# Three w1 chunks in the ring where there were four, and 1,728 fewer columns of one record loaded again

## The chip, the cores and the metric

The program runs on one core of one Trainium2 chip. The metric is device time in microseconds (us): 711.79 us is the median of three runs of the kernel before (711.76 to 711.85). Times inside the program come from one profiled execution.

## What is computed

Two layers are applied twice in turn to four tokens of 640 values: attention over a cached window (32 heads of 128, the last 1,024 keys and values of a cache of 4,096), then a dense layer of width 1,728 with a ReLU. Everything is float32. Cut to what matters:

```python
def _A_ref(x, k_cache, v_cache, wq, wo):        # k, v: the last W = 1024 of 4096 positions
    q = (x @ wq).reshape(B, Sq, Hq, Dh).transpose(0, 2, 1, 3)
    scores = jnp.einsum("bhqd,bhkd->bhqk", q, k) * (Dh ** -0.5)
    p = _softmax(scores, axis=-1)
    o = jnp.einsum("bhqk,bhkd->bhqd", p, v)
    return o.transpose(0, 2, 1, 3).reshape(B, Sq, Hq * Dh) @ wo

def _B_ref(x, w1, w2):
    h = jnp.maximum(jnp.einsum("bsd,df->bsf", x, w1), 0)
    return jnp.einsum("bsf,fd->bsd", h, w2)

x = x + _A_ref(_layernorm(x), A_k_cache, A_v_cache, A_wq, A_wo)   # round one
x = x + _B_ref(_layernorm(x), B_w1, B_w2)
x = x + _A_ref(_layernorm(x), A_k_cache, A_v_cache, A_wq, A_wo)   # round two, same weights and caches
x = x + _B_ref(_layernorm(x), B_w1, B_w2)
```

## The kernel before

All weights and caches of one head lie side by side as a record of 9,472 columns by 128 partitions: wq (640 columns), keys (4,096), values (4,096), wo (640). One column is 512 bytes over all partitions, so a record is 4.85 MB. The kernel streams records from memory into five slots of one record each. TensorE (PE) forms a head's query, its scores, its values and its share of the projection; VectorE (DVE) and ScalarE (ACT) do the softmax. After 32 heads the dense layer (`mlp`) runs on w1 (8,640 columns, five chunks of 1,728, each a block of 128 rows of the input) and w2 (54 tiles of 160 columns). Then the same again as round two.

Both rounds read the same records, so what is still on the chip at the end of round one isn't loaded again. Five records (heads 27 to 31) stay in the slots and come first in round two. A sixth (head 26, `SIXTH`) comes next; it lives in `ring`, a buffer of 9,152 columns beside the slots. Between its two uses, round one's w1 and w2 have to pass through the low columns of the same ring. The columns from `KEPT` (6,944) upwards are left alone; 1,056 columns just below `KEPT` (and 320 at the ring's start) are moved aside into PSUM (`put_by`, `lend`) and copied back later (`take_back` by ACT, in the dense layer; `put_back` by DVE, in round two). What lies below `HELD` (5,888) is overwritten and is loaded again, in the four pieces of `SIXTH_PIECES`.

What passes through the ring is the table `MLP_RING`: one entry for each load, with its quarters of a w1 chunk, its w2 tiles and the ring column where it starts. Every load is one DMA on the queue of SyncE (SP), which issues in the order of the list `items` and waits at each entry until the columns that it overwrites were last read (`pump`, `free`, `done`); the loads behind it wait too. A load that overwrites a w1 chunk waits for that chunk's last matmul. Four chunks fit before, at columns 0, 1,728, 3,456 and 5,184; the fifth takes the first one's place. Then come the w2 loads, the pieces of the sixth record, and the first loads of round two into the slots, each of which waits until PE has read what it overwrites.

PE's order is the order of the code. `busy(n)` is a filler: a product of one row with n columns whose result nobody reads. It writes columns 512 and up of `sc_ps[1]`; the 512 columns that `lend` put aside lie in the same tile `sc_ps[1]`, and `take_back` reads them there. In `mlp`, round one, there is a filler behind the tiles of w2 loads 1, 2 and 3 (counted from 0), and `take_back` comes behind load 2. Right behind the last w2 tile DVE transposes the new x, and PE starts on round two: the query of head 27 (`center`, `query`), then its scores.

All recorded operations have the line of one helper (`InOrder`, line 94), so the profile's rows are told apart by their tiles.

Of the kernel before, what the change touches and what calls it, by code (L numbers as in the profile page):

```python
# [2 lines left out]

# [12 lines left out]
B, D, H, DH, W, FF = 4, 640, 32, 128, 1024, 1728  # L41
# [20 lines left out]
SIXTH = H - NS - 1  # L62
RING = WO + 2 * FD
W1_COLS = KB * FF
KEPT = 4 * FF + 32
LENT = 512
BESIDE = KEPT - 192 - (512 - FD)
HELD = BESIDE - LENT

MLP_RING = [(4, 0, 0), (4, 0, FF), (4, 0, 2 * FF), (4, 0, 3 * FF), (4, 0, 0), (0, 10, 1728), (0, 11, 3328), (0, 11, 5088),  # L70
            (0, 10, 0), (0, 8, 1600), (0, 4, 2880)]

SIXTH_PIECES = [(3520, 5088), (5088, HELD), (0, 1600), (1600, 3520)]
FILL = [False, False, False, True]
W1_SLOT = [[0, 1], [2], [3], [4]]
W2_SLOT = [22, 14, 10, 4, 4]
# [25 lines left out]
def decode_kernel(ctx: ExitStack, tc: tile.TileContext, xf, rec, w, out):  # L102
# [65 lines left out]
    def home(h, r):  # L168

        if h == SIXTH:  # L170
            return "ring"
        return h % NS if not r or h >= LAST else (h + LAST) % NS
# [10 lines left out]
    def load(key, src, lo, hi, buf, col):  # L183
        buf, col = place(buf, col)
        items.append(([(key, lo, hi, col)] if key else [], src, lo, hi, buf, col))
# [33 lines left out]
    n = 0  # L219
    for quarters, tiles, col in MLP_RING:  # L220
        size = quarters * FQ + tiles * FD
# [3 lines left out]

    for lo, hi in SIXTH_PIECES:
        load(None, rec[:, SIXTH * REC:], lo, hi, "ring", lo)
# [19 lines left out]
    def pump():  # L247

        while items:
            parts, src, lo, hi, buf, col = items[0]  # L250
            if any(b == buf and x < col + hi - lo and col < y for b, x, y in live):
                return
            sp.dma_start(buffers[buf][:, col:col + hi - lo], src[:, lo:hi])
            live.append((buf, col, col + hi - lo))
            for key, x, y, c in parts:
                at.setdefault(key, []).append((x, y, buf, c))
            items.pop(0)
# [4 lines left out]
    def cols(key, lo, n):  # L262

        for x, y, buf, col in pieces(key):
            if x <= lo and lo + n <= y:
                return buffers[buf][:, col + lo - x:col + lo - x + n]
        raise KeyError((key, lo, n))

    def free(buf, a, b):
        rest = []  # L270
        for bb, u, v in live:
            if bb != buf or v <= a or b <= u:
                rest.append((bb, u, v))
            else:
                rest += [(bb, p, q) for p, q in ((u, a), (b, v)) if p < q]
        live[:] = rest

    def done(key, lo, hi):

        if key[0] == "rec" and key[1] == 0 and key[2] >= LAST:  # L280
            return
        if key == ("rec", 0, SIXTH):
            hi = min(hi, HELD)
        for x, y, buf, col in pieces(key):
            a, b = col + max(lo, x) - x, col + min(hi, y) - x
            if a < b:
                free(buf, a, b)
        pump()

    aside = acc[:, FD:], ring[:, BESIDE:BESIDE + 512 - FD]  # L290
    held = [(0, 0, REC - RING), (REC - RING, BESIDE + 512 - FD, KEPT)]
    lent = sc_ps[1][:, :LENT], ring[:, HELD:BESIDE]

    def put_by():

        for col, a, b in held:
            dve.tensor_copy(hold[:, col:col + b - a], ring[:, a:b])
            free("ring", a, b)
        free("ring", BESIDE, KEPT)
        pump()  # L300
# [7 lines left out]
    def take_back():  # L308

        assert not any(buf == "ring" and x < BESIDE and HELD < y for buf, x, y in live), live  # L310
        act.activation(*lent[::-1], AF.Copy)
        live.append(("ring", HELD, BESIDE))
# [10 lines left out]
    def busy(n, to=sc_ps[1][:, 512:]):  # L323

        pe.matmul(to[0:1, :n], ones, slot[home(LAST, 0)][:, K:K + n], start=True, stop=True)

    def centered_wq(h, ks):

        mean = sc_ps[1][:, 512:512 + DH]
        for k in ks:  # L330
            pe.matmul(mean, minus.to_broadcast([P, P]), cols(("rec", 0, h), WQ + k * DH, DH), start=(k == 0),
                      stop=(k == KB - 1))
        if ks[-1] == KB - 1:
            wq = cols(("rec", 0, h), WQ, D).rearrange("p (k d) -> p k d", d=DH)
            dve.tensor_tensor(wq, wq, mean.unsqueeze(1).to_broadcast([P, KB, DH]), op=OP.add)
# [27 lines left out]
    def deviation(bias, scale):  # L363

        pe.matmul(o_ps[:, 8:8 + B], ones.to_broadcast([P, P]), squares, start=True, stop=True)
        act.activation(rstds, o_ps[:, 8:8 + B], AF.Sqrt, bias=bias, scale=scale / D)

    def row_rstd(rows):

        dve.reciprocal(rstds, rstds)  # L370
        dve.tensor_tensor(mrt, rstds, rows, op=OP.mult)
        dve.tensor_reduce(rstd, mrt, op=OP.add, axis=AX.X)

    def xblock(k):
        return xT[:, 32 * k:32 * k + B]
# [58 lines left out]
    def picks(last, copy=None):  # L434
        o = outs[last].rearrange("p (c j) -> p c j", c=4)
        dve.tensor_tensor(o, o, of_block.unsqueeze(2).to_broadcast([P, 4, DH]), op=OP.mult)
        if copy:
            dve.tensor_copy(*copy)
        dve.tensor_reduce(on[last], o.rearrange("p c j -> p j c"), op=OP.add, axis=AX.X)
# [12 lines left out]
    def mlp(r):  # L452


        h_ps, front, back = sc_ps[0][:, :512], t_ps[:, :224], sc_ps[0][:, 512:768]
        key = ("w", r)
        turns = list(accumulate(quarters for quarters, _, _ in MLP_RING if quarters))
        for n in range(KB * NB):
            k, j = divmod(n, NB)
            pe.matmul(h_ps[32 * j:32 * j + B, :FQ], xblock(k), cols(key, n * FQ, FQ), start=(k == 0),  # L460
                      stop=(k == KB - 1))
            done(key, n * FQ, n * FQ + FQ)
            if n == NB - 1:
                deviation(eps, 1.0)
                if r == 0:
                    busy(256)
                row_rstd(pick)
            if r == 0 and n + 1 in turns[:-1]:
                i = turns.index(n + 1)
                if i in (1, 2):  # L470
                    centered_wq(LAST, (range(0, 2), range(2, KB))[i - 1])
                elif FILL[i]:
                    busy(512)
        act.activation(front, h_ps[:, :224], AF.Relu, scale=rstd)
        act.activation(back[:, :208], h_ps[:, 224:FQ], AF.Relu, scale=rstd)
        act.activation(back[:, 240:], h_ps[:, 416:FQ], AF.Relu, scale=rstd)
        dve.transpose(scratch[:, :224], front)
        dve.transpose(scratch[:, 224:], back)
        busy(512)
        busy(256)  # L480
        sizes = W2_SLOT if r else [tiles for _, tiles, _ in MLP_RING if tiles]
        first = 0
        for i, size in enumerate(sizes):
            for s in range(first, first + size):
                m, n = TILES[s]
                w2 = cols(key, W1_COLS + s * FD, FD)
                for part, q in ((m, n),) if m < 13 else ((13, n), (14, n + 2)):
                    pe.matmul(acc[32 * q:32 * q + B, :FD], hT[:, part, :B], w2,
                              start=False, stop=(s >= len(TILES) - NB), skip_group_check=True)
            if r == 0 and 0 < i < len(sizes) - 2:  # L490
                busy(512)
            done(key, W1_COLS + first * FD, W1_COLS + (first + size) * FD)
            if r == 0 and i == 2:
                take_back()
            first += size


    pump()
    pe.matmul(acc[:, :FD], ident, x_sb, start=True, stop=False, skip_group_check=True)
    for r in range(2):  # L500
# [11 lines left out]
        for n, h in enumerate(hs[:-2]):  # L512
            i = n - (H - late)
# [5 lines left out]
            if back:  # L519
                assert not any(buf == "ring" and x < KEPT and BESIDE < y for buf, x, y in live)  # L520
            picks(0, aside[::-1] if back else aside if r == 0 and h == SIXTH else None)
# [30 lines left out]
        for i in (late - 3, late - 1, late - 2) if late > 2 else (1,):  # L552
            project(r, hs[H - late + i], i, i == late - 2 or late == 2)
        center()
        mlp(r)
    dve.tensor_copy(x_sb, acc[:, :FD])
    sp.dma_start(out, x_sb)
# [38 lines left out]
```

## Time and profile before

| | |
|---|---|
| median of three runs | 711.79 us (711.76 to 711.85) |
| profiled execution, first to last instruction (span) | 710.5 us |
| between that span and the median of the runs | 1.3 us |
| PE, DVE, ACT busy | 72%, 46%, 14% of the span |
| DMA traffic | 302.64 MB, mean 426 GB/s |
| read from memory by the program's own loads | 302.00 MB |
| round one's dense layer | about 366 to 385 us |

The profile gives the profiled execution's span only; its whole device time isn't shown, so the runs' median stands beside the span. The rows of the windows view give a stretch of time (us from the span's start), its length, the busy time of PE, PE's weight load, DVE, ACT and POOL with the number of instructions, the granted clock of TensorE (1.00 is full speed), the busy share of the 16 DMA engines, and the GB/s that they moved. A DMA engine counts as busy from a packet's start to its end, also while the packet waits. "us to landing" runs from the issue on SP to the last of a load's bytes being reported. KB are 1,024 bytes.

### The profile page before, as it was taken

What the parts mean: (1) busy time and instruction counts of PE and PEld (TensorE: products, weight loads), DVE (VectorE), ACT (ScalarE), POOL (GpSimd) and SP (SyncE); (2) the same over time, 40 slices, a digit from 0 to 9 for tenths busy, and PEclk for the clock granted to TensorE, in tenths of its full rate; (3) what the DMA queues carried; (4) which work ended last, traced back from release to release, by engine and by line L of the source; (5) the groups of instructions that cost most, each with busy time, mean ns of one, the idle gap of its engine ahead of it and who ended that gap; (6) DMA issues with size and microseconds to landing.
All of it is one profiled execution on the core that took longest, in us unless ns stands there. A gap on an engine that the chain in (4) does not pass through costs nothing.

```text
span 710.5 us, 8690 instructions
## 1 busy us (share of the span) xinstructions
PE 513.6 (72%) x3706; PEld 202.8 (29%) x3706; DVE 323.3 (46%) x678; ACT 99.7 (14%) x211; POOL 1.1 (0%) x9
## 2 busy tenths in 40 slices
PE   3567686678584578857888898865686677576897
PEld 2132232232231223322223334331331322231423
DVE  3333353353452353546641777644352444253762
ACT  1100110011010110111121212201010111011111
POOL 0000000000000000000000000000000000000000
PEclk9957787677777776888999899977576677677899
DMA  9999999999999999999999999999999999999997
GB/s 381 463 409 451 415 442 443 414 442 444 424 429 440 434 429 421 435 425 430 424 416 403 421 435 428 438 434 448 429 445 427 428 442 430 427 442 406 431 423 292
DMA packets 13318, 302.64 MB, mean 426 GB/s; under 512 B 1488, under 2 KB 1760, under 8 KB 5216
## 3 DMA queue, kind: packets, MB, share of 16 engines
q1 hardware_dynamic: 13248, 302.08, 99.1%
q8 instruction: 29, 0.48, 0.2%
q14 instruction: 9, 0.07, 0.0%
q10 hardware_dynamic: 32, 0.01, 0.0%
HBM read 302.00 MB, written 0.08 MB: 425 GB/s over the span
## 4 chain that ended last, share of the span: by engine, by line
DMA 73%; PE 21%; DVE 4%; issue 1%; ACT 1%; SPq 0%; ACTq 0%; DVEq 0%
DMA slots<-rec 57%; PE sc_ps L94 11%; DMA ring<-w 8%; PE o_ps L94 7%; DMA ring<-rec 5%; PE acc L94 2%; DMA slots<-w 2%; DVE scratch L94 2%; DVE o_ps L94 1%; ACT oTs L94 1%; DVE small L94 0%; ACT sc_ps L94 0%; DVE turned L94 0%; SPq L94 0%; DVE ring L94 0%
## 5 line engine op out<-in xcount | busy, mean ns | idle before, releaser
L94 PE MATMUL sc_ps<-slots,qT 128*4 128x512 f32 x992 | 194.5, 869 | 37.4 <-DMA slots<-rec 36.4
L94 PE MATMUL sc_ps<-xT,slots 128*128 128x4 f32 x620 | 94.6, 279 | 99.8 <-DMA slots<-rec 99.2
L94 PE MATMUL o_ps<-slots,scratch 128*16 128x512 f32 x960 | 149.3, 693 | 2.4 <-DVE scratch L94 1.7
L94 DVE TENSOR_REDUCE small<-sc_ps 128x1 f32<-128x1024 f32 x64 | 78.3, 1224 | 156.9 <-PE sc_ps L94 156.9
L94 PEld LDWEIGHTS sc_ps<-xT,slots 128*128 128x128 f32 x620 | 89.2, 225 | 157.8 <-DMA slots<-rec 109.0
L94 ACT ACTIVATE sc_ps<-sc_ps,small 128x1024 f32<-128x1024 f32 (+1 forms) x68 | 71.1, 1046 | 342.2 <-DVE small L94 340.7
L94 DVE STREAM_TRANSPOSE turned<-sc_ps 128x1024 f32<-128x1024 f32 (+1 forms) x85 | 84.6, 996 | 0.7
L94 PEld LDWEIGHTS o_ps<-slots,scratch 128*16 128x16 f32 x960 | 34.5, 118 | 120.0 <-issue 107.6
L94 DVE TENSOR_TENSOR o_ps<-o_ps,of_block 128x512 f32<-128x512 f32 x62 | 43.4, 699 | 53.6 <-PE o_ps L94 52.3
L94 PEld LDWEIGHTS sc_ps<-slots,qT 128*4 128x4 f32 x992 | 32.3, 108 | 121.9 <-issue 64.9
L94 DVE TENSOR_TENSOR qT<-sc_ps,by_row 128x4 f32<-128x4 f32 x62 | 9.7, 156 | 114.1 <-PE sc_ps L94 114.1
L94 PE MATMUL acc<-slots,oTs 128*4 128x160 f32 x496 | 35.4, 368 | 19.2 <-ACT oTs L94 18.5
L94 DVE TENSOR_REDUCE scratch<-o_ps 128x128 f32<-128x512 f32 x62 | 42.9, 691 | 2.1
L94 ACT ACTIVATE oTs<-o_ps 128x4 f32<-128x4 f32 x64 | 11.1, 174 | 214.1 <-PE o_ps L94 214.1
L94 PE MATMUL o_ps<-pick,scratch 128*128 128x4 f32 x128 | 26.8, 280 | 15.9 <-DVE scratch L94 15.9
L94 PEld LDWEIGHTS o_ps<-pick,scratch 128*128 128x128 f32 x128 | 22.4, 218 | 21.4 <-DVE scratch L94 21.1
L94 DVE TENSOR_TENSOR scratch<-turned,by_row 128x128 f32<-128x128 f32 (+1 forms) x85 | 22.0, 259 | 3.2
L94 PE MATMUL sc_ps<-slots,small 128*1 128x512 f32 (+2 forms) x56 | 21.5, 486 | 0.0
L94 DVE TENSOR_SCALAR by_row<-of_batch,small 128x4 f32<-128x4 f32 x64 | 14.7, 230 | 2.2
L94 PEld LDWEIGHTS acc<-slots,oTs 128*4 128x4 f32 x496 | 6.9, 84 | 25.2 <-ACT oTs L94 23.5
L94 DVE STREAM_TRANSPOSE scratch<-small 128x32 f32<-128x32 f32 x64 | 12.9, 202 | 2.2 <-ACT sc_ps L94 2.2
L94 ACT ACTIVATION_READ_ACCUMULATOR sc_ps<-sc_ps,small 128x1 f32 x64 | 12.3, 193 | 0.0
(66 smaller groups left out, 103.7 us busy)
## 6 DMA issues: line engine op xcount, KB each, us to landing
slots<-rec SPq DMA_DIRECT2D x15, 7872.0 KB, 27.0
slots<-rec SPq DMA_DIRECT2D x8, 7936.0 KB, 31.5
slots<-rec SPq DMA_DIRECT2D x17, 2368.0 KB, 16.9
slots<-rec SPq DMA_DIRECT2D x4, 4736.0 KB, 25.9
slots<-rec SPq DMA_DIRECT2D x2, 4416.0 KB, 29.3
slots<-rec SPq DMA_DIRECT2D x7, 1024.0 KB, 19.7
ring<-w SPq DMA_DIRECT2D x8, 864.0 KB, 10.9
ring<-rec SPq DMA_DIRECT2D x1, 4576.0 KB, 36.2
```

Of the source, the lines that this page charges most:

```text
L94: r = build(*args, **kwargs)
```

## The change

Columns up to `KEPT` = 5,216 are now given to the stream, so three w1 chunks fit (at 0, 1,728 and 3,456) and the fourth waits for the first. The 1,056 columns that are moved aside lie at 4,160 to 5,216. Round two loads columns 0 to 4,160 of the sixth record again, in pieces of 1,600, 800, 1,120 and 640. The w2 loads hold 11, 10, 11, 11, 7 and 4 tiles (before: 10, 11, 11, 10, 8, 4), and `take_back` stands behind w2 load 3. PE gets two more fillers in round one: 512 columns behind the tiles of load 4, ahead of the last load's tiles, and 256 columns behind the last tile. The file is 25 lines shorter at the top, so line 94 is line 69 in it.

```diff
-KEPT = 4 * FF + 32
+KEPT = 3 * FF + 32
...
-MLP_RING = [(4, 0, 0), (4, 0, FF), (4, 0, 2 * FF), (4, 0, 3 * FF), (4, 0, 0), (0, 10, 1728), (0, 11, 3328), (0, 11, 5088),
-            (0, 10, 0), (0, 8, 1600), (0, 4, 2880)]
-
-SIXTH_PIECES = [(3520, 5088), (5088, HELD), (0, 1600), (1600, 3520)]
+MLP_RING = [(4, 0, 0), (4, 0, FF), (4, 0, 2 * FF), (4, 0, 0), (4, 0, FF), (0, 11, 2 * FF), (0, 10, 0), (0, 11, 1600),
+            (0, 11, 3360), (0, 7, 0), (0, 4, 1120)]
+
+SIXTH_PIECES = [(1760, 3360), (3360, HELD), (0, 1120), (1120, 1760)]
...
-            if r == 0 and 0 < i < len(sizes) - 2:
+            if r == 0 and 0 < i < len(sizes) - 1:
                 busy(512)
             done(key, W1_COLS + first * FD, W1_COLS + (first + size) * FD)
-            if r == 0 and i == 2:
+            if r == 0 and i == 3:
                 take_back()
             first += size
+        if r == 0:
+            busy(256)
```

SP's queue from the first w1 chunk to round two's first load into the slots, before (`w` is w1 and then w2, `rec` the records):

```order
L94 DMA ring<-w 128x1728 x5
L94 DMA ring<-w 128x1600
L94 DMA ring<-w 128x1760 x2
L94 DMA ring<-w 128x1600
L94 DMA ring<-w 128x1280
L94 DMA ring<-w 128x640
L94 DMA ring<-rec 128x1568
L94 DMA ring<-rec 128x800
L94 DMA ring<-rec 128x1600
L94 DMA ring<-rec 128x1920
L94 DMA slots<-rec 128x640
```

And with the change:

```order
L69 DMA ring<-w 128x1728 x5
L69 DMA ring<-w 128x1760
L69 DMA ring<-w 128x1600
L69 DMA ring<-w 128x1760 x2
L69 DMA ring<-w 128x1120
L69 DMA ring<-w 128x640
L69 DMA ring<-rec 128x1600
L69 DMA ring<-rec 128x800
L69 DMA ring<-rec 128x1120
L69 DMA ring<-rec 128x640
L69 DMA slots<-rec 128x640
```

The number of loads and the columns of w are the same; the four pieces of the record have 4,160 columns in place of 5,888.

PE from w2 load 3 to round two's first query, before, with what each row waits for (`acc<-ring,scratch` are the w2 tiles, `sc_ps<-slots,small` the fillers, `sc_ps<-xT,slots` the query of head 27; DMAHW is a load, Activation is ACT):

```order
L94 MATMUL acc<-ring,scratch 4x160 [waits DMAHW6_49]
L94 MATMUL acc<-ring,scratch 4x160 x9
L94 MATMUL sc_ps_73<-slots,small 1x512 [waits Activation_49]
L94 MATMUL acc<-ring,scratch 4x160 [waits DMAHW7_49]
L94 MATMUL acc<-ring,scratch 4x160 x7
L94 MATMUL acc<-ring,scratch 4x160 [waits DMAHW0_49]
L94 MATMUL acc<-ring,scratch 4x160 x3
L94 MATMUL sc_ps_72<-xT,slots 128x4 [waits DVE_49]
```

And with the change:

```order
L69 MATMUL acc<-ring,scratch 4x160 [waits DMAHW6_49]
L69 MATMUL acc<-ring,scratch 4x160 x10
L69 MATMUL sc_ps_73<-slots,small 1x512
L69 MATMUL acc<-ring,scratch 4x160 [waits DMAHW7_49]
L69 MATMUL acc<-ring,scratch 4x160 x6
L69 MATMUL sc_ps_73<-slots,small 1x512 [waits Activation_49]
L69 MATMUL acc<-ring,scratch 4x160 [waits DMAHW0_49]
L69 MATMUL acc<-ring,scratch 4x160 x3
L69 MATMUL sc_ps_73<-slots,small 1x256
L69 MATMUL sc_ps_72<-xT,slots 128x4 [waits DVE_49]
```

The filler that waits for ACT's `take_back` moved from behind w2 load 3 to behind load 4, right ahead of the last load's tiles, and a filler stands between the last tile and the query.

## The prediction

> **What bounds the kernel.** I read the page first: how full the DMA engines are, and what the chain that ended last is made of.
>
> ```profile
> span 710.5 us, 8690 instructions
> ...
> DMA  9999999999999999999999999999999999999997
> GB/s 381 463 409 451 415 442 443 414 442 444 424 429 440 434 429 421 435 425 430 424 416 403 421 435 428 438 434 448 429 445 427 428 442 430 427 442 406 431 423 292
> ...
> HBM read 302.00 MB, written 0.08 MB: 425 GB/s over the span
> ...
> DMA 73%; PE 21%; DVE 4%; issue 1%; ACT 1%; SPq 0%; ACTq 0%; DVEq 0%
> ```
>
> The DMA engines are 90% busy or more in every slice but the last, and the chain is DMA for 73%. So the time is about the bytes over the rate, and a byte that is not loaded is time saved, as long as the queue stays fed. Whether it does is read from the stretch that the change touches, the dense layer of round one and what follows it; the windows view, with 500 to 600 us as the steady state:
>
> ```profile
> 350.00:360.00 10.00, 8.86 (x58) 2.77 (x58) 6.91 (x18) 1.98 (x4) 0.00 (x0) 1.00 0.99 414
> 360.00:370.00 10.00, 8.40 (x82) 3.03 (x82) 3.52 (x12) 1.89 (x4) 0.00 (x0) 1.00 1.03 424
> 370.00:380.00 10.00, 8.10 (x80) 2.88 (x80) 1.69 (x3) 1.08 (x3) 0.00 (x0) 1.00 1.01 406
> 380.00:390.00 10.00, 8.90 (x101) 3.84 (x104) 1.33 (x7) 0.80 (x2) 0.00 (x0) 0.88 1.01 397
> 390.00:400.00 10.00, 8.04 (x62) 3.30 (x54) 7.34 (x20) 4.09 (x8) 0.00 (x0) 0.95 1.01 412
> 400.00:410.00 10.00, 9.08 (x68) 3.34 (x72) 6.96 (x16) 1.51 (x4) 0.00 (x0) 0.73 1.03 435
> ...
> 500.00:600.00 100.00, 74.29 (x470) 28.68 (x470) 40.87 (x79) 12.41 (x27) 0.00 (x0) 0.71 1.01 435
> ```
>
> Between 370 and 400 us the busy share says 1.01, yet the rate is 406, 397 and 412 GB/s where it is 435 later. Packets there are held open longer than their bytes need: some of the 16 engines already wait for work with a ring of four. 30 us at a mean of 405 in place of 435 are 2.1 us of transfer. This is the place where the change can lose what it saves.
>
> How the ring feeds the queue is seen in the chain of waits (start, length, what):
>
> ```profile
> 355.18 10.94 DMA ring<-w
> 366.12 0.14 issue
> 366.26 0.91 PE sc_ps L94 x8
> ...
> 367.22 7.14 DMA ring<-w
> 374.37 0.04 issue
> 374.41 0.95 PE sc_ps L94 x8
> ...
> 375.38 7.35 DMA ring<-w
> ...
> 443.23 18.13 DMA slots<-rec
> ```
>
> The first chunk lands at 366.12; PE reads it, and 1.10 us after the landing, at 367.22, the fifth chunk is issued into its place. It lands 7.14 us later, at 374.36. In these 8.24 us four chunks of 864 KB landed, one each 2.06 us, close to the 2.03 us that 884,736 bytes take at 435 GB/s.
>
> **The bytes.** The sixth record's four pieces shrink by 1,728 columns, 884,736 bytes; w1 and w2 are the same 17,280 columns in the same eleven loads, and four pieces stay four. At 435 GB/s that is **-2.03 us**. The lower end by a row, 397 GB/s, gives -2.23.
>
> **The ring of three.** A load into the ring is issued when the chunk three back (before: four back) has been read. One round is then 1.10 us from landing to issue, plus the fixed part of a load (everything but its bytes), plus 2.06 us of bytes, and it has to fit into three transfers, 6.18 us, where it had four, 8.24 us. It fits if the fixed part is no more than 6.18 - 1.10 - 2.06 = **3.02 us**. No row measures the fixed part in this stretch. Bounds are in the DMA issues (KB each, us to landing): the first load of the program, the output at the end, and the loads of w2.
>
> ```profile
> slots<-rec SPq DMA_DIRECT2D x1, 2368.0 KB, 8.3
> ...
> ring<-w SPq DMA_DIRECT2D x2, 880.0 KB, 7.2
> ring<-w SPq DMA_DIRECT2D x2, 800.0 KB, 7.4
> ...
> out<-scratch SPq DMA_DIRECT2D x1, 80.0 KB, 1.6
> ```
>
> The first load finds all engines empty: 8.3 us less 5.57 us for its bytes is 2.7 us. The output is 1.6 less 0.19, 1.4 us, but small and alone. From above, a w2 load of 880 KB lands after 7.2 us of which 2.07 are bytes, so its fixed part is under 5.1. The first load is the nearest kind, a large load for which every engine waits, but nothing else moved then; the fall to 406 GB/s with four chunks says that in traffic some engines wait for longer than that. I take 3.3 us, a quarter of the way from 2.7 to 5.1. That is 0.28 us over per round. From the fourth chunk to the last w2 load eight loads hang on a load three back, 2.7 rounds: **+0.75 us**, between 0 (2.7 us, it fits) and +5.6 (5.1 us).
>
> The Trainium skill (DMA: Bandwidth & Descriptors, section "Anatomy of one DMA — SWDGE (gpsimd) path") has about 2.0 us fixed plus the bytes at 436 GB/s, for the other kind of queue. By it the ring of three would cost nothing. The first load above took 8.3 us where that gives an estimate of 7.6, so the trace is slower than the page.
>
> **The fillers and round two's first loads.** The timeline of w2's end and of round two's start:
>
> ```profile
> 382.47 0.60 ACT L94 ACTIVATE ring<-sc_ps 128x512 f32<-128x512 f32 x1 [5.94 <-PE sc_ps L94]
> ...
> 382.77 0.85 PE L94 MATMUL acc<-ring,scratch 128*4 128x160 f32 x18 [0.34 <-DMA ring<-w]
> 383.33 0.59 PE L94 MATMUL sc_ps<-slots,small 128*1 128x512 f32 x1
> ...
> 383.76 0.59 PE L94 MATMUL sc_ps<-slots,small 128*1 128x512 f32 x1
> 384.31 1.22 PE L94 MATMUL acc<-ring,scratch 128*4 128x160 f32 x24
> 385.90 1.28 PE L94 MATMUL sc_ps<-xT,slots 128*128 128x4 f32 x10 [0.37 <-DVE xT L94]
> ...
> 387.43 1.80 PE L94 MATMUL sc_ps<-slots,qT 128*4 128x512 f32 x8
> ...
> 389.69 1.66 PE L94 MATMUL sc_ps<-slots,qT 128*4 128x512 f32 x8
> ...
> 392.97 1.04 PE L94 MATMUL sc_ps<-slots,qT 128*4 128x512 f32 x8 [0.42 <-DVE qT L94]
> ```
>
> `take_back` on ACT waits for a filler and is waited for by the next one. Before, ACT was done at 383.07, ahead of that filler at 383.33. Now it stands between the filler behind load 3 and the one behind load 4, and the last load's tiles are queued behind that on PE. From the landing of load 3 the path is its tiles (0.56, as 382.77 to 383.33), a filler (1.02, 383.33 to 384.35), ACT (0.60), a filler (1.02) and the last tiles (0.4, a third of the 1.22 us for 24): 3.6 us. By the bytes alone the last tiles could be done after 560 KB and 320 KB more, 2.07 us, and 0.4: 2.5. So PE starts round two 1.1 us later than the loads allow; the last filler (256 columns, about half of 1.02) stands where PE idled 0.37 us for DVE and adds some 0.2. Together 1.3.
>
> Against it stands the clock:
>
> ```profile
> 385.00:386.50 1.50, 1.09 (x18) 0.71 (x14) 0.62 (x3) 0.00 (x0) 0.00 (x0) 1.00 0.98 394
> 386.50:387.50 1.00, 0.97 (x13) 0.88 (x16) 0.22 (x2) 0.00 (x0) 0.00 (x0) 1.00 1.07 400
> 387.50:391.00 3.50, 3.50 (x18) 0.66 (x18) 0.99 (x6) 1.19 (x2) 0.00 (x0) 0.51 1.00 381
> ```
>
> Right behind the query, from 387.5 to 391, the granted clock is 0.51, and the two groups of scores take 1.80 and 1.66 us where the same eight take 1.04 at full clock (392.97). If the added work keeps the clock up, PE has 0.76 us back by the first scores and 1.38 by the second. I take that it does; then PE is where it was, within 0.1, at the second.
>
> Who waits for PE there is SP: round two's loads into the slots go out as PE reads what they overwrite.
>
> ```profile
> 389.28 0.33 SPq L94 DMA_DIRECT2D slots<-rec  x1
> ...
> slots<-rec SPq DMA_DIRECT2D x4, 1024.0 KB, 7.6
> slots<-rec SPq DMA_DIRECT2D x1, 1344.0 KB, 8.2
> ```
>
> The 1,344 KB load, the fourth of them, has 8.2 us to landing. Its bytes take 3.16, its fixed part 3.3; 1.7 us of queue cover it. The change takes 2.03 us of queue away ahead of it, so 0.3 us are not covered: **+0.3 us** with the clock up, 0 with a fixed part of 2.7, +1.7 with the clock down (1.38 more). Later loads have more cover (the one at 443.23 in the chain, 4,736 KB by the program and so 11.1 us of bytes, takes 18.13), and from 400 us the rate is back at 435. The chunk rounds don't add here, since they make the queue and PE late alike. The eight or so added PE instructions among 8,690 are the fillers, priced above. The tail behind the last load is untouched.
>
> **The sum** is -2.03 + 0.75 + 0.3 = **-1.0 us**, against the profiled execution's span of 710.5: 709.5. The runs' median lies 1.3 us above that span, outside first and last instruction, and I take that as unchanged: **710.8 us**.
>
> **Rivals.**
>
> *The ring of three costs nothing.* With a fixed part of 2.7 us, as in the first load, a round is 5.9 us against 6.18, and 8.2 - 3.16 - 2.7 leaves 2.3 us of cover for the 2.03 that go. Then only the bytes count: 711.8 - 2.03 = 709.8. For it speaks the only row of a large load with empty engines, and that chunks landed at full pace with four; against it the 2.1 us that 370 to 400 lose already. Should PE be faster by the clock, some of these come back too, down to 709.3.
>
> *The ring and the late PE eat more than the bytes* (slower). One mechanism: the fixed part in traffic, from w1's fourth chunk on, with the clock down again in round two's first scores. The Trainium skill (TensorE: Matmul & The Clock Gate, Part 1) says that the clock is judged in free-running windows of 3.4 us, so the fillers may only move the slow window onto other scores; the trace has the slow stretch of 3.5 us, and no run here shows what fillers do to it. In rows: at a fixed part of 3.9 us, midway between the bounds, the rounds cost 0.88 x 2.7 = 2.4, and the 1,344 KB load has 1.1 us of cover for 2.03 + 1.38, which is +2.3: together +2.7, 714.5. It is slower by over 0.2% from a fixed part of about 3.6 on (2.7 x 0.58 + 2.0 - 2.03 = +1.5). Against it: with four chunks the loop closed exactly at the transfer time, so no chunk waited there.
>
> *The bytes were hidden anyway.* The chain's last DMA in the dense layer ends at 382.73 and the next one it names starts at 443.23; between them it runs over PE, DVE and ACT. If PE sets the pace of round two's start, the queue only becomes shorter: 711.8. Against it: the DMA share from 380 to 410 is 1.01 to 1.03, and the load at 443.23 waits 7 us behind others.
>
> That the change doesn't do what it says can be left out: the queue's order shows the smaller pieces.
>
> **Chances.** The forecast 0.42 (its own range 710.3 to 712.0), the free ring 0.36 (709.3 to 710.3), the slower case 0.14, hidden bytes 0.08. The forecast stands ahead of the free ring since the fall of the rate with four chunks is seen, and a fixed part under 3.02 us in traffic is not. A measurement of this kernel tells 0.2% (1.4 us, that is 710.4 and 713.2) from no change. Faster by more than that: the free ring and the forecast's lower edge, 0.40. Within: the rest of the forecast and the hidden bytes, 0.46. Slower: 0.14. The range that should hold 8 in 10 is 709.2 to 713.0: the lower end adds the faster PE to the free ring, the upper end lets in the beginning of the slower case.
>
> **What will show it.** HBM read falls by 0.88 MB to 301.1 MB. In the chain, a chunk issued three back lands after 5.1 us if the ring is free, after 5.4 with a fixed part of 3.3, after 6 and more in the slower case; the last w2 load lands near 385.0 if free, 385.8 by the forecast. The rate from 370 to 400 falls from 405 towards 390. The first scores of round two take about 1.04 us each if the fillers hold the clock, and the row of `take_back` ends right ahead of a filler. The load of 1,344 KB lands about 1.0 us earlier than before (2.0 if free), and every later one by the same. Wrong would be a rate from 370 to 400 as before with the same time, or loads after 410 us that land no earlier though the w loads kept pace.

## The result, and the profile after

The changed kernel is slower: 716.88 us against 711.77 us (medians), a ratio of 1.0075 (95% interval 1.0053 to 1.0096). In a second comparison, told below, it was 1.0044 (1.0032 to 1.0057). The forecast was 710.8 us, and its range ended at 713.0. The profile below is of the fastest of the four executions, 715.09 us; no trace shows what made the other three longer (716.10 to 719.45).

The page of the changed kernel:

```profile
span 713.3 us, 8699 instructions
...
GB/s 382 462 404 450 444 412 441 444 419 435 440 427 427 443 431 425 432 422 428 424 379 362 379 435 428 445 425 450 437 426 435 440 422 432 447 423 416 430 423 292
...
HBM read 301.12 MB, written 0.08 MB: 422 GB/s over the span
...
DMA 71%; PE 21%; DVE 4%; ACT 1%; issue 1%; another core or an unknown queue 0%; SPq 0%; ACTq 0%; DVEq 0%
```

The bytes fell as the change says, from 302.00 to 301.12 MB. What changed for the worse are three slices in the middle of the row of rates, 379, 362 and 379 GB/s, where the kernel before had 416, 403 and 421. The windows view of these slices:

```profile
360.00:370.00 10.00, 8.61 (x83) 3.04 (x82) 3.79 (x12) 1.89 (x4) 0.00 (x0) 1.00 0.96 382
370.00:380.00 10.00, 6.99 (x70) 2.38 (x74) 1.69 (x3) 1.08 (x3) 0.00 (x0) 1.00 0.99 367
380.00:390.00 10.00, 7.74 (x105) 3.20 (x93) 0.62 (x3) 0.60 (x1) 0.00 (x0) 1.00 0.96 361
390.00:400.00 10.00, 8.44 (x70) 3.33 (x70) 6.21 (x18) 3.04 (x5) 0.00 (x0) 1.00 0.92 328
400.00:410.00 10.00, 8.66 (x80) 4.42 (x84) 8.63 (x21) 2.75 (x6) 0.00 (x0) 0.91 1.02 421
```

From 370 to 400 us the rate is 352 GB/s on the mean (367, 361, 328); it was 405, and the forecast had some 390. The busy share hardly shows it (0.96, 0.99, 0.96, 0.92), since a packet that is held open counts as busy. From 400 to 410 us it is 421 where it was 435, and from 410 to 430 the two kernels are alike (434 and 430). So the loss lies between 360 and 410 us, in the two places that the prediction names. To see how much in each, the stretch is cut at 386 us, about where w2 ends (its last load lands at 385.03 us before and at 387.38 after). The kernel before, then the changed one:

```profile
360.00:386.00 26.00, 21.43 (x237) 7.71 (x237) 5.62 (x18) 3.57 (x8) 0.00 (x0) 1.00 1.02 413
386.00:410.00 24.00, 21.09 (x152) 8.67 (x156) 15.23 (x41) 5.80 (x11) 0.00 (x0) 0.82 1.02 416
```

```profile
360.00:386.00 26.00, 19.76 (x213) 7.19 (x213) 5.48 (x15) 2.97 (x7) 0.00 (x0) 1.00 0.98 373
386.00:410.00 24.00, 20.69 (x186) 9.18 (x184) 15.46 (x42) 6.39 (x12) 0.00 (x0) 0.96 0.96 370
```

A stretch loses its length times (435 - rate)/435. Before, that is 1.3 us up to 386 and 1.0 behind it; after, 3.7 and 3.6. So the ring's stretch lost 2.4 us more, and round two's start 2.5 us more, together 4.9. Less the 2.03 us of the bytes that is +2.9 us; the spans of the two profiles differ by 2.8. Both places count, and each is larger than its term in the prediction (0.75 and 0.3).

The chain of waits of the changed kernel from w1 to round two's first scores (start, length, what):

```profile
370.52 0.95 PE sc_ps L69 x8
...
371.49 6.25 DMA ring<-w
...
377.88 1.02 PE acc L69 x22
...
378.92 6.29 DMA ring<-w
...
385.25 0.99 PE acc L69 x22
...
387.13 0.60 ACT ring L69
...
391.00 1.04 PE sc_ps L69 x8
```

Two w2 loads of 880 KB take 6.25 and 6.29 us from issue to landing. 2.07 of these are bytes, so 4.2 us are the fixed part, where the prediction took 3.3. It is more than the wait behind the load ahead, which by the trace had landed 3.9 us after the issue in both cases. Most of the time is lost at two other loads, issued at 369.41 and 376.43 us. They landed 2.82 and 3.15 us behind the load ahead of them, with 2.03 and 2.07 us of bytes. Next to it stands PE's timeline from the landing of w2 load 3 on:

```profile
385.25 0.99 PE L69 MATMUL acc<-ring,scratch 128*4 128x160 f32 x22 [0.54 <-DMA ring<-w]
386.07 1.02 PE L69 MATMUL sc_ps<-slots,small 128*1 128x512 f32 x2
...
387.78 0.59 PE L69 MATMUL sc_ps<-slots,small 128*1 128x512 f32 x1 [0.41 <-ACT ring L69]
...
389.46 1.28 PE L69 MATMUL sc_ps<-xT,slots 128*128 128x4 f32 x10
```

It is the order that the prediction described: tiles, a filler, ACT, a filler, the last tiles. The query starts at 389.46 where it started at 385.90. By the trace the last w2 load landed at 387.38 (before: 385.03), so 2.35 us of these 3.56 are late loads, and 1.2 us are fillers and ACT.

### The profile page after: what moved, and what is told of

Read it like the earlier page. It is cut to its first block, busy times and chain, and to the rows that moved or that the text cites. A ratio compares the mean times of both kernels' runs of the same rounds, so it can differ in the third digit from the quotient of the medians.

```text
span 713.3 us, 8699 instructions
## 1 busy us (share of the span) xinstructions
PE 509.6 (71%) x3710; PEld 204.0 (29%) x3710; DVE 323.3 (45%) x678; ACT 99.6 (14%) x211; POOL 1.1 (0%) x9
## 2 busy tenths in 40 slices
DMA packets 13318, 301.75 MB, mean 423 GB/s; under 512 B 1488, under 2 KB 1760, under 8 KB 5216
## 3 DMA queue, kind: packets, MB, share of 16 engines
HBM read 301.12 MB, written 0.08 MB: 422 GB/s over the span
## 4 chain that ended last, share of the span: by engine, by line
DMA 71%; PE 21%; DVE 4%; ACT 1%; issue 1%; another core or an unknown queue 0%; SPq 0%; ACTq 0%; DVEq 0%
DMA slots<-rec 62%; PE sc_ps L69 11%; PE o_ps L69 7%; DMA ring<-w 7%; PE acc L69 3%; DMA slots<-w 2%; DVE scratch L69 2%; DVE o_ps L69 2%; ACT oTs L69 1%; DVE small L69 0%; ACT sc_ps L69 0%; SPq L69 0%; DVE turned L69 0%; ACT ring L69 0%
## 5 line engine op out<-in xcount | busy, mean ns | idle before, releaser
L69 PE MATMUL sc_ps<-slots,qT 128*4 128x512 f32 x992 | 187.3, 844 | 44.6 <-DMA slots<-rec 43.6
L69 PE MATMUL sc_ps<-slots,small 128*1 128x512 f32 (+2 forms) x60 | 23.1, 486 | 0.4 <-ACT ring L69 0.4
```

The costliest lines, as they stand in the source:

```text
L69: r = build(*args, **kwargs)
```

## The experiments

Two theories stood at the outset. *Loop and cover*: three chunks in flight, and the shorter queue behind w2, do not cover the time that a load needs to start. *Late PE*: the fillers and `take_back` hold up round two's start. Times of the kernel before in these comparisons are 711.8 to 712.0 us.

**The parts alone.** The bytes on the ring of four:

```diff
-SIXTH_PIECES = [(3520, 5088), (5088, HELD), (0, 1600), (1600, 3520)]
+SIXTH_PIECES = [(3520, 5088), (5088, HELD), (0, 1152), (1600, 2240)]
```

> The kernel before, with its ring of four chunks and its fillers, but 1,728 columns of the sixth record are not loaded again (two of the four pieces are shorter; round two then computes with whatever stands there, so its result is not the reference's). Loop theory (three loads in flight don't cover the fixed part of a load, about 4 us in traffic): the ring of four is not the cause, so most of the bytes is won, 709.7 to 710.8 us: 711.8 - 2.03, and up to 1.1 back because the shorter queue no longer covers round two's first loads. Late-PE theory (the fillers and take_back cost the time): 709.7. If the bytes were hidden in any case: 711.8.

Measured: 711.0 us, ratio 0.9987 (0.9978 to 0.9996). Of 2.03 us about 0.9 are won, on the ring of four. Its windows:

```profile
360.00:386.00 26.00, 21.62 (x239) 7.89 (x239) 5.85 (x18) 3.57 (x8) 0.00 (x0) 1.00 1.02 414
386.00:410.00 24.00, 21.10 (x163) 8.70 (x167) 15.05 (x40) 5.80 (x11) 0.00 (x0) 0.86 1.00 399
```

Up to 386 us nothing changed (414 and 413); behind it the rate fell from 416 to 399, which is 0.9 us more lost. So the shorter queue alone lets the engines run dry at round two's start.

The ring of three and the changed fillers, on the bytes of before:

```diff
-KEPT = 3 * FF + 32
+KEPT = 4 * FF + 32
```

> The changed kernel with KEPT back at four chunks: the ring stays three chunks wide, the fillers stay, but 5,888 columns of the sixth record are loaded again as before. Loop theory: the loss of the rounds stays, (1.10 + 4.1 + 2.06 - 6.18) x 2.7 = 2.9 us, and the bytes that come back stand behind the w2 loads, where they cover round two's first loads: 714.7 us, and not the 716.9 + 2.03 = 718.9 that would follow if every byte cost its transfer. Late-PE theory: with 2 us more of queue in front of them round two's first loads cover a PE that is 1 us late, so little is lost: 711.8 to 712.5.

Measured: 716.44 us, ratio 1.0069 (1.0049 to 1.009). The ring of three, together with the fillers that came with it, costs some 4.6 us, and with the bytes given back the kernel is no slower than 716.88 (0.7 us slower than the 715.72 of the second comparison, below). The size is above the loop theory's 714.7, and far from the late-PE theory's 712.

```profile
360.00:386.00 26.00, 18.78 (x190) 6.61 (x190) 5.20 (x15) 2.97 (x7) 0.00 (x0) 1.00 0.96 362
386.00:410.00 24.00, 20.48 (x198) 9.59 (x202) 14.56 (x40) 6.40 (x12) 0.00 (x0) 0.99 1.00 399
```

Its loss is mostly in the ring's stretch, 362 GB/s or 4.4 us (before 1.3). Round two's start, with 5,888 columns behind w2, has 399 where the changed kernel has 370; that is 2.0 us lost (before 1.0).

PE's part alone, on the kernel before (a filler behind w2 load 4, `take_back` behind load 3, 256 columns behind the last tile):

```diff
-            if r == 0 and 0 < i < len(sizes) - 2:
+            if r == 0 and 0 < i < len(sizes) - 1:
...
-            if r == 0 and i == 2:
+            if r == 0 and i == 3:
```

> The kernel before with only the PE part of the change: a filler also behind w2 load 4, take_back behind load 3, and a 256-column filler behind the last tile; ring, loads and bytes are as before. Late-PE theory: PE starts round two 1.3 us later and the loads behind it are late by that: 713.1. Cover theory: 5,888 + 640 columns, 7.7 us, stand behind the last w2 load, as much as is needed, and the fillers hold the clock in the first scores: 711.8 (711.4 to 712.4).

Measured: 712.27 us, ratio 0.9996 (0.9988 to 1.0005). PE's query starts 0.7 us later than before:

```profile
386.58 1.28 PE L94 MATMUL sc_ps<-xT,slots 128*128 128x4 f32 x10
```

With the whole queue of before behind w2 this costs nothing that the runs can tell. So the late-PE theory has fallen as the cause by itself. The next run took PE's wait for ACT out of the changed kernel; its fillers stayed:

```diff
-                busy(512)
+                busy(512, *([sc_ps[0]] if i > 3 else []))
...
-            busy(256)
+            busy(256, sc_ps[0])
```

> The changed kernel, but the filler behind w2 load 4 and the one behind the last tile write into another tile (sc_ps[0]), so that nothing on PE waits for take_back on ACT ahead of the second head's query. Late-PE theory: PE is about 0.7 us earlier at round two's start and most of the loss of 7.1 us against 709.8 comes back: 711 to 713. Loop theory: the loads are late before PE is, so it is worth 0 to 0.7 us: 716.2 to 716.9.

Measured: 715.71 us, ratio 1.005 (1.0038 to 1.0062). This is below the 716.2 that the loop theory gave as its lowest, but the changed kernel itself, once more, was at the same time:

> The changed kernel itself once more, beside the others and in more rounds, for the sum of its parts. If the parts only add, -0.9 (bytes alone), +4.6 (ring alone) and +0.3 (PE part alone): 715.9 us. Cover theory: with the ring of three the bytes win nothing, since the queue runs dry behind w2 in any case: 716.4 or more, no better than the ring alone.

Measured: 715.72 us, ratio 1.0044 (1.0032 to 1.0057). So the wait for ACT is worth nothing that can be measured; the two intervals overlap and are about 0.9 us wide to each side. The parts add, as far as the runs can tell: -0.9 + 4.6 = +3.7 against a measured +3.9 here and +5.1 in the first comparison. The 0.3 us of PE's part, which the expectation added once more, is in the 4.6 already, since that run has the fillers. The expectation of the cover theory, 716.4 or more, was missed. Whether the bytes win anything on the narrow ring stays open: the ring with all bytes has 1.0049 to 1.009, the changed kernel 1.0032 to 1.0057 and 1.0053 to 1.0096.

**Cover at round two's start.** If every column taken from the queue there is lost again, leaving out twice as many wins no more:

```diff
-SIXTH_PIECES = [(3520, 5088), (5088, HELD), (0, 1600), (1600, 3520)]
+SIXTH_PIECES = [(3520, 4480), (5088, HELD), (0, 352), (1600, 1920)]
```

> The kernel before with 3,456 columns of the sixth record not loaded again (2,432 are; round two computes with whatever stands in the others, so its result is not the reference's), twice what the run with 1,728 fewer left out. Cover theory (what stands in the queue behind the last w2 load covers the time until round two's first 2,048-column load delivers; with 1,728 fewer it already ran dry there for 2.4 us): every further column is lost again, 711.0 us (710.5 to 711.5), as with 1,728 fewer. Byte theory (each column saves its transfer, the first 0.9 us were cut short by something else): 711.0 - 2.05 = 708.9.

Measured: 711.27 us, ratio 0.9987 (0.9973 to 1.0001); the byte theory's 708.9 is out of reach.

```profile
360.00:386.00 26.00, 22.07 (x246) 8.28 (x240) 6.97 (x21) 4.17 (x9) 0.00 (x0) 1.00 1.01 409
386.00:410.00 24.00, 20.84 (x186) 9.66 (x185) 17.60 (x43) 7.01 (x13) 0.00 (x0) 1.00 0.94 373
```

The rate behind 386 us goes 416, 399, 373 as the columns go 5,888, 4,160, 2,432; 373 means 3.4 us lost, 2.4 more than before. The step behind it can be counted. By the trace, the last w2 load landed at 385.03 before and at 384.85 with 4,160 columns. Behind it stand the record's pieces and the 640-column load, 7.7 us of bytes before and 5.65 then, so that by its bytes alone the queue ends at 392.7 and 390.5. The next load, 2,048 columns, can be issued only when PE has done the first four products of round two: 389.28 and 388.36. In the second case it has this row (KB, us from issue to landing):

```profile
slots<-rec SPq DMA_DIRECT2D x1, 1024.0 KB, 7.3
```

7.3 us, of which 2.4 are bytes: it lands at 395.63, and its bytes on the last engine start at 393.2, 2.7 us behind the end of the queue. Fifteen engines have it by 393.71, 0.8 us later than a full queue would; the other 1.9 us are one engine's, and what held that one up isn't known. In the changed kernel the last w2 load lands at 387.38, the queue ends by its bytes at 393.0, the load is issued at 392.10 and lands at 398.00, 2.6 us later than a full queue would have it.

**The start of a load.** To make its loss larger, w1 gets two chunks of ring, and w2 comes in loads of 10 tiles:

```diff
-MLP_RING = [(4, 0, 0), (4, 0, FF), (4, 0, 2 * FF), (4, 0, 0), (4, 0, FF), (0, 11, 2 * FF), (0, 10, 0), (0, 11, 1600),
-            (0, 11, 3360), (0, 7, 0), (0, 4, 1120)]
+MLP_RING = [(4, 0, 0), (4, 0, FF), (4, 0, 0), (4, 0, FF), (4, 0, 0), (0, 10, FF), (0, 10, 0), (0, 10, 1600),
+            (0, 10, 0), (0, 10, 1600), (0, 4, 0)]
...
-SIXTH_PIECES = [(1760, 3360), (3360, HELD), (0, 1120), (1120, 1760)]
+SIXTH_PIECES = [(3200, HELD), (1600, 3200), (640, 1600), (0, 640)]
```

> The ring-only kernel (5,888 columns loaded again, as before) with w1 in two chunks of the ring instead of three and w2 in six loads of 10, 10, 10, 10, 10 and 4 tiles on the same 3,456 columns. Two transfers are 4.12 us; a round is 1.10 + f + 2.06. Loop theory with f of 3.1 to 4.3 us, as the loads three back showed: 2.1 to 3.3 us over, nine loads hang on one two back, 4.5 rounds, so 10 to 15 us above the kernel before: 721 to 727. If f is 2 us and the ring of three lost its time elsewhere: 4.5 x 1.04 = 4.7 above, 716.5.

Measured: 721.32 us, ratio 1.0119 (1.0102 to 1.0137), at the lower end of the loop theory's range. Its chain of waits:

```profile
367.31 4.42 DMA ring<-w
...
372.75 5.73 DMA ring<-w
...
379.89 4.25 DMA ring<-w
...
385.21 4.27 DMA ring<-w
```

A load of 800 KB takes 4.25 us, with 1.88 of bytes; the first one, of 864 KB, 4.42 with 2.03. So the fixed part is **2.4 us** when the engines stand empty. But the one at 372.75, of 864 KB, takes 5.73, a fixed part of 3.7. What differs is seen in the trace's landings, one for each of the 16 engines (us):

```
two chunks, issued 376.67, 800 KB    380.50 ... 380.83 380.92    spread 0.4
two chunks, issued 382.08, 800 KB    386.03 ... 386.93 387.28    spread 1.3
three, issued 369.41, 864 KB         373.60 ... 374.66 375.42    spread 1.8
three, issued 371.49, 880 KB         376.30 ... 377.73 377.74    spread 1.4
four (before), issued 360.84, 864 KB 369.16 ... 372.27 372.31    spread 3.1
```

Of the nine w loads of this kernel that wait for a place in the ring, four land on all engines within about 0.4 us and the first within 0.5; the other four, and the waiting w loads of the ring of three, land 1 us and more later on some engines than on others, and a load has landed when the last engine has. With a deep queue (the last row) the engines are 3 us apart too, but the last one keeps the pace of the bytes: the next loads land at 374.37 and 376.25, 2.06 and 1.88 us on.

**Smaller loads.** More loads in flight on the same three chunks: w1 in ten half chunks, w2 in eleven loads.

```diff
+MLP_RING = [(2, 0, 0), (2, 0, 864), (2, 0, 1728), (2, 0, 2592), (2, 0, 3456), (2, 0, 4320), (2, 0, 0), (2, 0, 864), (2, 0, 1728), (2, 0, 2592), (0, 5, 3456), (0, 6, 4256), (0, 5, 0), (0, 5, 800), (0, 5, 1600), (0, 6, 2400), (0, 5, 3360), (0, 6, 4160), (0, 5, 0), (0, 3, 800), (0, 3, 1280)]
...
+            if r == 0 and n + 1 in (8, 12):
+                centered_wq(LAST, range(0, 2) if n + 1 == 8 else range(2, KB))
```

> The changed kernel's columns and bytes (KEPT of three chunks, 4,160 columns loaded again), but w1 comes in ten loads of half a chunk and w2 in eleven loads of 3 to 6 tiles; the filler stands behind every second w2 load and PE does not wait for take_back. Loop theory: six loads in flight, so a round of 0.6 + 4.1 + 1.03 = 5.7 us fits into 6.18 and the loss of the rounds is gone; the bytes are won: 710.5 us (709.7 to 711.5). If the fixed part is time that each load holds the engines, so that loads cost by their number, or by the late-PE theory: 716 or more.

Measured: 713.96 us, ratio 1.0029 (1.002 to 1.0038). Part of the loss comes back, not all; both theories had another number. The rate up to 386 us is 378, hardly better than 373, and 378 behind it (370). In its trace a half chunk waited for PE, which stood in `centered_wq`; so that was moved away:

```diff
-            if r == 0 and n + 1 in (8, 12):
-                centered_wq(LAST, range(0, 2) if n + 1 == 8 else range(2, KB))
...
+            if r == 0 and i in (1, 3):
+                centered_wq(LAST, range(0, 2) if i == 1 else range(2, KB))
```

> The half-chunk loads on three chunks of ring, with centered_wq moved from between w1's chunks to behind w2 loads 1 and 3, so that PE reads each half at once. Loop theory: with six small loads in flight and PE prompt, the w loads lose under 1 us where the first half-chunk kernel lost 2.7 (there loads waited for PE behind centered_wq); what is left is the cover at round two's start, 2.5 to 3 us, against -2.05 of bytes: 712.6 us (712.0 to 713.3). If the number of loads or the narrow ring itself is what costs: 714.0 as with the first half-chunk kernel.

Measured: 714.94 us, ratio 1.0039 (1.0026 to 1.0052), a miss: moving `centered_wq` won nothing. What the expectation had left out is PE's first step in w1:

```profile
366.67 0.38 PE L68 MATMUL o_ps<-pick,small 128*128 128x4 f32 x2
...
367.33 0.97 PE L68 MATMUL sc_ps<-ring,xT 128*4 128x432 f32 x8
```

The first half chunk landed at 365.15, but PE reads it from 367.33, when the statistics of x (the product at 366.67) are ready. Until then nothing is issued; the next half chunk goes out at 368.35, and the sixth one ends the queue at 370.61. That is 2.3 us of cover, and whole chunks had 3.0 (issued 367.46, queue until 370.48). With x arriving when it does, it is the ring's bytes that cover the start, and cutting them finer gains little. That the 21 smaller w loads cost something by their number (there were 11) isn't ruled out: no run has them on the ring of four.

Seven half slots, a compromise with 5,024 columns loaded again, and the same with an earlier round two:

```diff
+KEPT = 7 * FF // 2 + 32
...
+SIXTH_PIECES = [(4160, HELD), (1120, 2560), (2560, 4160), (0, 1120)]
```

> Half-chunk loads of w1 in seven half slots (KEPT of three and a half chunks, 5,024 columns loaded again), w2 in eleven loads, centered_wq moved from between w1's chunks to behind w2 loads 1 and 3 so that PE reads w1 without a stop, take_back behind w2 load 4. Loop and cover theory: seven small loads in flight leave little of the rounds' loss (under 1 us where the ring of three lost 2 to 3.5), 864 columns fewer are -1.02 us, and 5,024 + 640 columns are 6.7 us of cover where 7 to 8 are needed: 711.3 us (710.5 to 712.5). If the number of loads costs: 713 or more.

```diff
-    for i, lo, hi in ((0, 0, K), (0, K, K + VH), (0, K + VH, V),
+    for i, lo, hi in ((0, 0, K), (0, K, K + 1024), (0, K + 1024, K + VH), (0, K + VH, V),
...
-            if r == 0 and i in (5, 6, 8, 9):
+            if r == 0 and i in (5, 7):
```

> The kernel with seven half slots, with fillers only behind w2 loads 5 and 7 (before: 5, 6, 8 and 9) and round two's first key load cut in two, each half issued when its two 512-column products are done. Cover theory: PE starts round two up to 0.9 us earlier and the first key load is issued 0.3 us earlier, so the 2 us lost behind the last w2 load shrink by about 1: 711.6 us (711.0 to 712.3). If the clock falls in the first scores, as in the kernel before: 712.8, unchanged.

Measured: 712.77 us, ratio 1.001 (0.9997 to 1.0022), and 713.07 us, ratio 1.0007 (0.9998 to 1.0016). Neither is faster than the kernel before: the seven half slots just miss the 712.5 that ended the expectation. The second kernel came near the number of its rival (712.8) by luck: the clock in its first scores did not fall (1.00 from 386 to 400 us), and its rate was lower up to 386 us (377 against 401). No version that computes the whole result beat the kernel before.

**What delays one engine.** Instructions come over the same DMA engines; the page lists 29 packets of 16 KB for them. In both profiles of the changed kernel such a packet at about 381 us stands beside a third w2 load of which one or two engines were 1.0 to 1.2 us late. Products of PE at the program's start move the packets, so these are PE's:

```diff
+    for _ in range(32):
+        pe.matmul(sc_ps[1][0:1, :1], ones, ones, start=True, stop=True)
```

> The changed kernel with 32 one-column products on PE at the start of the program, where PE waits 13 us for the first load. PE's instructions come in packets of 16 KB on the same 16 DMA engines; in the profiles of the changed kernel such a packet at 381.0 and 381.3 us stands beside a landing of the third w2 load (issued at 376.2 and 376.4) that is 1.1 us late on one or two engines alone. The added instructions move every later packet ahead, that one to about 377. Packet theory: the engine that is late alone moves with it, to a load that lands around 378 to 381, and the third w2 load loses under 0.4; the time stays within 1.5 us of 716. Issue theory: the third w2 load is late by about 1.1 as before, whatever the packet does.

> The kernel before with the same 32 products at the start. Packet theory: with four chunks in flight an engine that a packet delays has up to 3 us of lead over the last one, so that moving the packets changes little: 711.8 us (711.2 to 712.5), and no w load is late by over 0.4 on one engine.

Measured: 715.94 us, ratio 1.0061 (1.0047 to 1.0075), and 711.84 us, ratio 0.9998 (0.9989 to 1.0006). In the changed kernel the packets moved to 368.4 and 385.8 us (the expectation had one at about 377), and none was left between 374 and 384. The third w2 load, issued at 376.80, still landed 1.0 us later than its bytes behind the load ahead (1.1 with the packet beside it), now with six engines late together: the packet theory has fallen for it. Where the packet went, it did show: the last w2 load landed on fifteen engines by 387.23 us and on the last one at 388.48. That engine's packets of the load start at 386.77 us, as the instruction packet ends (385.83 to 386.78). The row of the window from 385 to 388 us (packets, MB, share of 16 engines) has that packet:

```profile
q8 instruction: 1, 0.02, 2.0%
```

So a packet on one engine cost that load 1.3 us, with a short queue. On the ring of four no w load was over 0.3 us later on one engine than on the other fifteen with the packets moved. What else makes some engines finish a load 1 us and more behind the others stays open.

## Why the prediction was wrong

**The ring of three** is the step that failed first. Its mechanism and its limit, 3.02 us, are as the runs show. The term that was mis-sized is the fixed part. It was taken as 3.3 us, "a quarter of the way from 2.7 to 5.1"; the changed kernel's loads measured 4.2 (4.0 and 4.3 at the two loads where most was lost). The prediction's own formula then gives (1.10 + 4.2 + 2.06 - 6.18) x 2.7 = 3.2 us in place of 0.75. The profile of the changed kernel lost 2.4 us more than before in that stretch, and the ring with its fillers cost 4.6 in all. The argument for the lower end, the first load of the program, was a load that found everything empty. In that state the two-chunk run measured 2.4 us. The Trainium skill's 2.0 us (DMA: Bandwidth & Descriptors, section "Anatomy of one DMA — SWDGE (gpsimd) path"), which are for the other kind of queue, are near it. Neither speaks of the last of 16 engines in traffic, and that one sets the landing. The rate of 406 GB/s with four chunks was already the sign, and the prediction gave it little weight. The witness that it offered was also misjudged: the first chunk issued three back landed after 5.14 us, "free", and the loads behind it after 6.0 and 6.25.

**Round two's first loads** failed too: +0.3 was forecast, 2.5 us were lost. The cover was counted at the 1,344 KB load, the fourth in the row, with 3.3 us fixed. The loads that decide stand ahead of it. When the first one of 1,024 KB is issued, 1.3 us behind the 640-column load, the queue had 3.4 us left by its bytes before (392.7 less 389.28), and 0.9 with the change (393.0 less 392.10): 2.0 us of bytes are gone, and 0.5 us by which PE answers later behind the last w2 load (4.7 against 4.25 us). The load's own fixed part was 3.5 us (5.90 less 2.41). The trace has the loss even earlier: behind the last w2 load, the 1,120-column piece and the 640-column load each landed about 1.0 us later behind the load ahead than their bytes take, and the first two 1,024 KB loads together 1.0. In the second comparison's profile of the changed kernel it is 0.5, 0.6 and 1.4. So the queue ran dry even before the first 1,024 KB load. The pieces, too, wait until PE has read the w2 columns that they overwrite (the last two went out at 387.45 and 389.15), and the prediction did not count that. The runs with 1,728 and 3,456 columns fewer show the loss without any ring of three: of 2.03 us and of 4.06 us saved, 0.9 and 0.7 are left. The load of 1,344 KB, which was to land 1.0 us earlier, landed 2.0 us later (404.31 against 402.31).

**The bytes** were right as a transfer (-0.88 MB), and wrong as a gain (0.9 us alone in place of 2.03), for the reason just given.

**The fillers.** PE's path was priced well: 1.2 us more from the last landing to the query, against 1.3 forecast. With the whole queue behind w2 it costs nothing (0.9996 alone). With the shorter queue it may: these 1.2 us are then missing from the cover, and no run leaves the fillers out of the changed kernel. The run without the wait for ACT took about 0.5 of them away, less than the runs can tell apart. The clock did what was forecast, 1.04 us for each of the first two groups of scores, but the fillers need not be the reason. With the fillers of the kernel before, the run with 1,728 columns fewer shows, in its chain of waits:

```profile
387.26 1.04 PE sc_ps L94 x8
...
388.62 1.01 PE sc_ps L94 x8
```

The slow scores (1.80 and 1.66 us) were seen in one execution of the kernel before; in three profiles of other kernels with the same fillers there (1,728 and 3,456 columns fewer, and 32 products at the start) the clock from 386 to 392 us was 1.00. The Trainium skill (TensorE: Matmul & The Clock Gate, Part 1) says that the windows in which the clock is judged run freely, so that it varies from run to run; the profiles agree. A gain of 1.38 us should not have been counted from one of them.

**The span and the time.** 1.3 us were added to the span. The changed kernel's profiled execution took 715.09 us with a span of 713.3, which is 1.8 us; other runs show 1.7 to 1.8. The kernel before showed its span without its own time, so 0.5 us of error came in there.

**The slower rival** (0.14) had the fixed part almost right (3.9) and the point from which it decides (3.6). Its 714.5 us were still below the 715.72 and 716.88 measured. Its other half, a clock that is down again, did not come. It was held unlikely since with four chunks "the loop closed exactly at the transfer time". That was a load which landed behind a full queue, and says nothing of how long it would take to start without one.

## What to carry to other kernels

A ring of buffers is deep enough when what is in flight covers the start of a load on its slowest engine in traffic (here 4.2 us, against 2.4 us when all engines are empty), and that figure must come from loads that really waited. Bytes that need not be loaded are a gain only as long as they were not what kept the engines busy while the next load could not yet be issued: count, from the last load that PE waits for, the bytes behind it against the first load that PE's answer releases. A granted clock or an end time that stands in a single profile should not carry a term of a sum.

## What had not been expected

The busy share of the DMA engines stayed at 0.92 to 0.99 while they lost up to a quarter of their rate (328 of 435 GB/s), so a dry queue is read from the rate, not from the share. And an instruction packet of 16 KB, about 0.9 us long, held up one engine's load by 1.3 us when the queue was short. With a deep queue such packets came as often and left no mark of more than about 0.3 us on the w loads. They are not always harmless there: in the profile of the kernel before, the 800 KB piece of the record issued at 383.80 landed on fifteen engines by 389.83 us and on the last one at 391.24, and that engine's packets of it begin at 388.79, as an instruction packet of 8 KB ends.
